# Decode attention on one core: two heads of K or V per DMA transfer, eight heads per softmax batch

## The chip, the core and the metric

One NeuronCore of a Trainium2 chip runs the whole kernel. The metric is device time in microseconds (us) of one execution, as the median of several runs. The core has five engines with a program each: TensorE (PE in the profile, its weight loads PEld) for matmuls, VectorE (DVE), ScalarE (ACT), GpSimd (POOL) and SyncE (SP), which here only issues DMA transfers. Sixteen DMA engines move data from HBM into the on-chip memory SBUF, which has 128 partitions; matmuls write to PSUM.

## The reference

A decoder block for four sequences with one new token each. x is 4 x 576.

```python
q = layernorm(x) @ wq                      # 32 query heads of 128
k = k_cache[:, :, Sk - W:, :]              # 4 x 16 KV heads, last W = 4096 of 16384 positions
v = v_cache[:, :, Sk - W:, :]
p = softmax(q @ k.T * 128 ** -0.5)         # two query heads share a KV head
h = x + (p @ v) @ wo
n = layernorm(h)
out = h + (relu(n @ W_gate) * (n @ W_up)) @ W_down   # F = 4608
```

All tensors are bf16. Per KV head the window of K is 4096 x 128 values, 1 MB, and it lies in one piece in HBM; the same holds for V. There are 64 KV heads (4 sequences x 16), so K and V are 128 MiB (134.2 million bytes) of the 159.6 million that the kernel reads; the rest are the five weight matrices and x.

## The kernel before

The order of the work is written out by hand. Each engine has its own program, and a small scheduler (class Sched) turns named events into semaphore waits.

**SP** issues every large transfer in one fixed list, in order. Before each it waits for whoever used the buffer last, so a wait holds up everything behind it in the list. The list is: wq in five pieces (L205 to L208); then for m = 0, 1, 2 ... K of head m and V of head m - 5 (L209 to L213; VLEAD is 5); then wo (L214), W_gate and W_up (L218 to L227) and W_down (L230 to L236). K goes through a ring of 6 buffers and V through one of 10, in the SBUF tensor `pool`; a buffer has 4608 columns of bf16. wq occupies the first five V buffers. A K or V transfer is 1 MB: 128 partitions with 8 KB each, and partition p holds positions 32p to 32p + 31 of one head (L195 to L203). A K buffer comes free with the transpose of that head, event ("TR", i), a V buffer with the last matmul on it, ("PV", i).

**DVE** transposes each K head in 32 x 32 blocks of 4-byte words into one of three buffers kT (`tr`, L376). It waits for the K transfer and, from the fourth on, for the matmuls that read the kT buffer before.

**PE** computes scores (`qk`, L497): eight matmuls of 512 columns per head, with a stationary operand qz that holds the queries of the head in its own columns and zeros elsewhere, so four heads (a batch, NB = 4) accumulate into the same 128 x 1024 of PSUM (`sc`, two of them in turn), row 32g + 2r + h for head r of the batch and query h.

For a **batch** DVE takes the maximum over the row (`rmax`, L384), POOL takes the maximum over partitions (L268), DVE makes the bias (`fbias`, L391), ACT writes the exponentials P (L314, two instructions of 512 columns), DVE transposes P (`trp`, L397) and ACT casts it to bf16 as `prob` (L321). PE then multiplies prob with V (`pv`, L514): eight matmuls of 512 columns per head with eight rows of output. In PE's program the PV of head j stands after the scores of head j + 6 (PVLAG, L539). ACT copies the batch's result out of PSUM (L301), and PE picks the right blocks out of it (`ext`, L526). ACT fills qz for the batch after next (`qzero`, L285).

Before the first head there is a chain of setup. POOL clears qz (L254) and then builds an identity matrix (L255). DVE makes masks from it (L345 to L363), ACT the normalised x (L281), PE its transpose (L476) and then q; the first transpose of K stands behind this in DVE's program (L413), and the second behind the copies of q (L415 to L417).

After the last head come wo, the second layernorm, the gate and up matmuls (each waits for its own weights) and the down matmuls. W_down lands on the place of K and wo buffers, so its transfers wait for the last wo matmul (event "ATTN", L234).

Of the kernel before, what the change touches and what calls it, by code (L numbers as in the profile page):

```python
# [12 lines left out]
B = 4  # L13
# [6 lines left out]
T = WIN // 128  # L20
# [3 lines left out]
NPAIR = B * KVH  # L24
NB = 4
NBATCH = NPAIR // NB
# [3 lines left out]
SLOT = 4608  # L30
NKS = 6
NVS = 10
NSLOT = NKS + NVS
# [3 lines left out]
PVLAG = 6  # L37
# [63 lines left out]
def bass_sequential_preLN__sliding_block_cached__glu_gated_reglu__decode_kernel(  # L101
# [12 lines left out]
    with ExitStack() as es:  # L114
# [4 lines left out]

        pool = sb("pool", [128, NSLOT, SLOT], BF16)  # L120
        kT = sb("kT", [128, NKT, WIN // 2], FP32)
# [19 lines left out]
        qz = sb("qz", [128, 2, NB, 4, 128], BF16)  # L141
        mask = sb("mask", [128, 4, 2 * NB], FP32)
        selT = sb("selT", [128, 4, 2 * NB], FP32)
        rmx = sb("rmx", [128, 2], FP32)
        pmax = sb("pmax", [128, 2, 2 * NB], FP32)
        bcm = sb("bcm", [128, 2, 2 * NB], FP32)
        t8 = sb("t8", [128, 2 * NB], FP32)
# [5 lines left out]
        prob = sb("prob", [128, 3, NB, T, 2], BF16)  # L153
# [22 lines left out]

        rings = {"K": [list(range(NKS)), 0], "V": [list(range(NKS, NSLOT)), 0]}
        slot_user = {}
        transfers = []
        slot_of = {}  # L180

        def add(name, ring, consumer, make, fixed=None):
            if ring is not None:
                slots, i = rings[ring]
                s = slots[i % len(slots)]
                rings[ring][1] += 1
                free = slot_user.get(s)
                slot_user[s] = consumer
                key = f"slot{s}"
            else:  # L190
                s, free, key = fixed, None, "fix_" + str(name).replace("'", "").replace("(", "").replace(")", "").replace(", ", "_")
            slot_of[name] = s
            transfers.append((name, key, free, lambda e, s=s: make(e, s)))

        def kv(cache, i):  # L195
            b, kvh = divmod(i, KVH)
            return cache[b, kvh, SK - WIN:SK, :].rearrange("(p t) d -> p (t d)", p=128)

        def add_K(i):
            add(("K", i), "K", ("TR", i), lambda e, s: e.dma_start(out=pool[:, s, 0:WIN], in_=kv(A_k_cache, i)))  # L200

        def add_V(i):
            add(("V", i), "V", ("PV", i), lambda e, s: e.dma_start(out=pool[:, s, 0:WIN], in_=kv(A_v_cache, i)))  # L203

        for c in range(4):  # L205
            add(("wq", c), "V", "QMM", lambda e, s, c=c: e.dma_start(out=pool[:, s, 0:H * DH], in_=A_wq[c * 128:(c + 1) * 128, :]))
        add(("wq", 4), "V", "QMM", lambda e, s: e.dma_start(out=pool[:, s, 0:H * DH // 2],
                                                            in_=A_wq[512:576, :].rearrange("r (u n) -> (r u) n", u=2)))  # L208
        for m in range(NPAIR + VLEAD):  # L209
            if m < NPAIR:  # L210
                add_K(m)
            if m >= VLEAD:
                add_V(m - VLEAD)  # L213
        for g in range(NWO):  # L214
            add(("wo", g), "K", "ATTN",
                lambda e, s, g=g: e.dma_start(out=pool[:, s, :].rearrange("p (q x) -> p q x", q=2),  # L216
                                              in_=A_wo[g * 1024:(g + 1) * 1024, :].rearrange("(q p e) n -> p q (e n)", q=2, e=4)))
        for c in range(4):  # L218
            for kind, W in (("wg", B_W_gate), ("wu", B_W_up)):
                add((kind, c), "V", None,  # L220
                    lambda e, s, c=c, W=W: e.dma_start(out=pool[:, s, 0:F], in_=W[c * 128:(c + 1) * 128, :]))

        s4 = rings["V"][0][rings["V"][1] % NVS]
        for u, (kind, W) in enumerate((("wg", B_W_gate), ("wu", B_W_up))):
            transfers.append(((kind, 4), f"gu4_{u}", slot_user[s4],
                              lambda e, u=u, W=W: e.dma_start(out=pool[:, s4, u * HALF:(u + 1) * HALF],
                                                              in_=W[512:576, :].rearrange("r (u n) -> (r u) n", u=2))))  # L227
        wd_sb = pool[:, 0:NKS, :].rearrange("p s x -> p (s x)")[:, 0:FC * D].rearrange("p (g x) -> p g x", g=NG)
        WD = [(0, GD * JJ), (GD * JJ, 2 * GD * JJ)] + [(g * JJ, (g + 1) * JJ) for g in range(2 * GD, NG - 1)] + [(FC - JJ, FC - 1), (FC - 1, FC)]
        for k, (f0, f1) in enumerate(WD):  # L230
            g0, j0 = divmod(f0, JJ)
            g1, nj = (f1 // JJ, JJ) if f1 - f0 >= JJ else (g0 + 1, f1 - f0)
            transfers.append((("wd", k), f"wd{k}", "ATTN",
# [8 lines left out]
        def prog_sync(S):  # L242
            for name, key, free, make in transfers:
                S.dma("sync", make, key, deps=[free], name=land(name))
            S.dma("sync", lambda e: e.dma_start(out=out.rearrange("b s d -> (b s) d"), in_=out_sb[:, :]), "outdma",
                  deps=["OUT0", "OUT1"], name="STORED")
            S.wait("sync", "STORED")
# [24 lines left out]
        def prog_act(S):  # L272
# [12 lines left out]
            def qzero(n):  # L285
                b, q = divmod(n, 4)
                for g in range(4):
                    deps = []
                    if g == 0:
                        deps = ["D_QR", "QZ0"] if n < 2 else [("QK", NB * (n - 2) + NB - 1)]  # L290
                    src = bass.AP(tensor=qrep, offset=32 * g * 4 * H * B + 8 * q * B + b, ap=[[4 * H * B, 32], [2 * B, NB], [H * B, 4], [B, 2]])
                    dst = bass.AP(tensor=qz, offset=32 * g * 2 * NB * 512 + (n % 2) * NB * 512 + 32 * g,
                                  ap=[[2 * NB * 512, 32], [512 + 2, NB], [128, 4], [1, 2]])
# [11 lines left out]
            for n in range(NBATCH):  # L305
                for half in range(2):
                    deps = []
                    if half == 0:
# [5 lines left out]
                    S.op(a, lambda e, n=n, half=half: e.activation(  # L314
                        out=P[:, half * 512:(half + 1) * 512], in_=sc[n % 2][:, half * 512:(half + 1) * 512], func=ACT.Exp,
                        scale=SCALE, bias=bias[:, n % 2:n % 2 + 1], accum_out=rs2[:, n % 2, half:half + 1]),
                        deps=deps, name=("EXP", n) if half else None, signal=half == 1)
                deps = [("TRP", n)]
                if n >= 3:
                    deps.append(("PV", NB * (n - 3) + NB - 1))  # L320
                S.op(a, lambda e, n=n: e.copy(out=prob[:, n % 3, :, :, :],  # L321
                                              in_=probT[:, :, 0:2 * NB].rearrange("p t (r h) -> p r t h", h=2)), deps=deps, name=("CMP", n))
# [13 lines left out]
        def prog_dve(S):  # L336
# [17 lines left out]
            for x in range(2):  # L354
                S.op(v, lambda e, x=x: e.memset(pb[PVB + x], 0.0), name=f"PVZ{x}")  # L355
            S.op(v, lambda e: e.tensor_reduce(out=mask[:, 0, :], in_=ident_b[:, :].rearrange("p (r u) -> p u r", u=2 * NB), axis=AX.X, op=ALU.add),
                 name="M0")
            S.op(v, lambda e: e.tensor_reduce(out=mask[:, 3, :], in_=bass.AP(tensor=ident_b, offset=0, ap=[[128, 128], [1, 2 * NB], [32, 4]]),
                                              axis=AX.X, op=ALU.add), name="M3")
            S.op(v, lambda e: e.tensor_scalar(out=mask[:, 1, :], in0=mask[:, 0, :], scalar1=2 * BIG, scalar2=-BIG, op0=ALU.mult, op1=ALU.add),  # L360
                 deps=["M0"], name="M1")
            S.op(v, lambda e: e.tensor_scalar(out=mask[:, 2, :], in0=mask[:, 0, :], scalar1=-2 * BIG, scalar2=BIG, op0=ALU.mult, op1=ALU.add),
                 name="M2")  # L363
            S.op(v, lambda e: e.reciprocal(out=st1[:, 5:6], in_=st1[:, 4:5]), deps=["A_STD"], name="D5")
# [11 lines left out]
            def tr(i):  # L376
                deps = [land(("K", i))]
                if i >= NKT:
                    deps.append(("QK", i - NKT))
                src = pool[:, slot_of[("K", i)], 0:WIN].bitcast(FP32).rearrange("p (t c k) -> p c t k", c=2, k=32)  # L380
# [3 lines left out]
            def rmax(n):  # L384
                S.op(v, lambda e: e.tensor_reduce(out=rmx[:, n % 2:n % 2 + 1], in_=sc[n % 2][:, :], axis=AX.X, op=ALU.max),  # L385
                     deps=[("QK", NB * n + NB - 1)], name=("RMAX", n))
# [4 lines left out]
            def fbias(n):  # L391
                S.op(v, lambda e: e.scalar_tensor_tensor(out=t8[:, :], in0=bcm[:, n % 2, :], scalar=-SCALE, in1=mask[:, 2, :],  # L392
# [4 lines left out]
            def trp(n):  # L397
                S.op(v, lambda e: e.transpose(out=probT[:, :, :].rearrange("p t j -> p (t j)"), in_=P[:, :]),  # L398
                     deps=[("EXP", n)] + ([("CMP", n - 1)] if n >= 1 else []), name=("TRP", n))
                b, q = divmod(n, 4)  # L400
                S.op(v, lambda e: e.tensor_tensor(out=rs1[:, n % 2:n % 2 + 1], in0=rs2[:, n % 2, 0:1], in1=rs2[:, n % 2, 1:2], op=ALU.add),  # L401
                     name=("RS1", n))
                S.op(v, lambda e: e.tensor_scalar(out=rowsum[:, b, 8 * q:8 * q + 8], in0=mask[:, 3, :], scalar1=rs1[:, n % 2:n % 2 + 1],
                                                  scalar2=None, op0=ALU.mult), deps=[("RS1", n)], name=("RSUM", n))

            def norm(b):
# [3 lines left out]
                     deps=[("RS", b), ("EXT", 4 * b + 3)], name=("NORM", b))  # L410

            for i in range(NPAIR):
                tr(i)  # L413
                if i == 0:
                    S.op(v, lambda e: e.tensor_copy(out=qT_sb[:, :], in_=pb[QB][:, 0:H * B]), deps=["QMM"], name="D_QT")  # L415
                    S.op(v, lambda e: e.tensor_copy(out=qrep[:, :, :].rearrange("p c x -> p (c x)"), in_=pb[QR]), deps=["QREP"], name="D_QR")  # L416
                    S.op(v, lambda e: e.tensor_copy(out=selT[:, :, :].rearrange("p t (r h) -> p t r h", h=2),  # L417
                                                    in_=bass.AP(tensor=ident_f, offset=0, ap=[[128, 128], [2, 4], [32, NB], [1, 2]])),
                         deps=["IDF"], name="SELT")
                n, pos = divmod(i, NB)  # L420
                if pos == NB - 1:
                    rmax(n)
                if pos == 0 and n >= 1:
                    fbias(n - 1)
                if pos == 1 and n >= 1:
                    trp(n - 1)
# [38 lines left out]
        def prog_pe(S):  # L465
# [73 lines left out]
            for i in range(NPAIR + PVLAG):  # L539
                if i < NPAIR:  # L540
                    qk(i)
# [100 lines left out]
```

## Time and profile before

| what | value |
|---|---|
| median of 3 runs | 389.33 us (389.22 to 389.44) |
| the profiled execution, its time | 389.34 us |
| its span in the profile | 387.6 us |
| bytes read from HBM | 159.58 MB |
| busy: PE, DVE, ACT, POOL | 301.1, 204.6, 60.1, 10.7 us |
| 64 transposes of K, mean of one | 2305 ns |
| 512 score matmuls, 512 PV matmuls, mean of one | 416 ns, 393 ns |
| a K or V transfer, from issue to landing (median) | 26.1 us, 26.9 us |

The span is the profile's own; 1.7 us of the execution's time lie around it. The strip of 40 slices shows each engine's busy share in tenths, and below it what the DMA engines moved in GB/s, so each slice is 9.7 us. The page's share of busy time counts a matmul from its start to its modelled end, so several overlap and PE's number is the union. "Releaser" names what ended an engine's wait. The lists of packets count every piece that a DMA engine moved: one for each partition's contiguous run, and a 4-byte one for each engine and transfer, which sets the semaphore.

### The profile page before, as it was taken

To read this page: it belongs to the slowest core of one execution; us is meant where nothing else is said; L and a number is where in the kernel's file an instruction comes from. 1 tells how busy PE (TensorE), PEld (TensorE's weight loads), DVE (VectorE), ACT (ScalarE), POOL (GpSimd) and SP (SyncE) were. 2 spreads that over 40 slices of the span, in tenths; PEclk is the share of its full clock that TensorE was granted. 3 is DMA by queue.
4 is the path that set the end of the run, shared out by engine and by line. 5 is a ranking of instruction groups with operands and counts; after the bars stand their busy time and mean duration, and the time that the engine had idled before them with its cause. 6 is when DMAs were issued, how large, how long until landed. Compare 5 with 4: busy or idle time off the path is not lost.

```text
span 387.6 us, 4471 instructions
## 1 busy us (share of the span) xinstructions
PE 301.1 (78%) x1906; PEld 131.3 (34%) x1906; DVE 204.6 (53%) x228; ACT 60.1 (16%) x173; POOL 10.7 (3%) x28
## 2 busy tenths in 40 slices
PE   0078779797979797979787878796879798774477
PEld 0053224242424242324232323242323233364344
DVE  0265967658483856574748575656566665011000
ACT  4020212111111111111111111111111111200000
POOL 3000000000000000000000000000000000000000
PEclk9999699999989998989999999899989989875559
DMA  8999999999999999999999999999999999999995
GB/s 322 419 419 423 423 421 418 420 423 420 423 419 420 424 421 422 420 420 421 421 424 421 418 424 421 424 417 421 421 421 422 423 421 419 414 418 421 418 412 203
DMA packets 23524, 159.88 MB, mean 413 GB/s; under 512 B 2505, under 2 KB 2641, under 8 KB 5585
## 3 DMA queue, kind: packets, MB, share of 16 engines
q1 hardware_dynamic: 23496, 159.59, 99.3%
q8 instruction: 15, 0.25, 0.3%
q14 instruction: 5, 0.03, 0.0%
q10 hardware_dynamic: 8, 0.00, 0.0%
HBM read 159.58 MB, written 0.00 MB: 412 GB/s over the span
## 4 chain that ended last, share of the span: by engine, by line
DMA 55%; PE 26%; DVE 12%; issue 4%; SPq 1%; ACT 0%; POOL 0%; POOLq 0%
DMA pool<-in_A_k_cache_dram 42%; PE sc L469 15%; PE pb L469 11%; DVE kT L382 8%; DMA pool<-in_B_W_down_dram 7%; DMA pool<-in_A_wo_dram 6%; DVE rmx L385 2%; SPq L216 1%; DVE pmax L387 0%; DVE pb L355 0%; ACT qz L294 0%; ACT xn_bf L281 0%; DVE sel L346 0%; PE pb L476 0%; DVE qrep L416 0%
## 5 line engine op out<-in xcount | busy, mean ns | idle before, releaser
L382 DVE STREAM_TRANSPOSE kT<-pool 128x2048 f32<-128x2048 f32 x64 | 147.2, 2305 | 59.5 <-DMA pool<-in_A_k_cache_dram 59.3
L469 PE MATMUL sc<-kT,qz 128*128 128x512 bf16 x512 | 137.8, 416 | 44.3 <-DVE t L392 33.0
L469 PE MATMUL pb<-pool,prob 128*8 128x512 bf16 x512 | 120.2, 393 | 0.0
L469 PEld LDWEIGHTS sc<-kT,qz 128*128 128x128 bf16 x512 | 47.0, 101 | 130.6 <-DVE t L392 40.5
L469 PEld LDWEIGHTS pb<-pool,prob 128*8 128x8 bf16 x512 | 38.9, 88 | 73.7 <-issue 28.2
L314 ACT ACTIVATE P<-sc,bias 128x512 f32<-128x512 f32 x32 | 21.7, 683 | 160.6 <-DVE bias L394 160.6
L385 DVE TENSOR_REDUCE rmx<-sc 128x1 f32<-128x1024 f32 x16 | 19.6, 1225 | 47.0 <-PE sc L469 47.0
L398 DVE STREAM_TRANSPOSE probT<-P 128x1024 f32<-128x1024 f32 x16 | 19.3, 1205 | 1.5 <-ACT P L314 1.5
L469 PEld LDWEIGHTS pb<-selT,cp 128*128 128x128 f32 x128 | 16.6, 191 | 6.6 <-ACT cp L301 4.2
L469 PE MATMUL pb<-selT,cp 128*128 128x8 f32 x128 | 15.4, 247 | 3.2 <-ACT cp L301 3.2
L301 ACT COPY cp<-pb 128x512 f32<-128x512 f32 x16 | 9.4, 586 | 53.5 <-PE pb L469 53.5
L469 PE MATMUL pb<-hnT,pool 128*128 128x4 bf16 x288 | 8.8, 167 | 9.8 <-DMA pool<-in_B_W_up_dram 5.2
L476 PE MATMUL pb<-ident_b,xn_bf 4*128 4x4 bf16 (+1 forms) x5 | 0.4, 175 | 19.6 <-ACT xn_bf L281 19.6
L294 ACT COPY qz<-qrep 32x32 bf16<-32x32 bf16 x64 | 13.9, 217 | 7.6 <-DVE qrep L416 7.0
L268 POOL PARTITION_ALL_REDUCE bcm<-pmax x16 | 5.9, 368 | 304.4 <-DVE pmax L387 304.4
L321 ACT CAST prob<-probT 128x256 bf16<-128x256 f32 x16 | 6.6, 414 | 44.6 <-DVE rs L401 44.6
L469 PEld LDWEIGHTS pb<-hnT,pool 128*128 128x128 bf16 x288 | 8.2, 104 | 10.3 <-DMA pool<-in_B_W_up_dram 5.4
L460 DVE TENSOR_TENSOR hhT<-pb,gate_sb 128x144 bf16<-128x144 f32 x1 | 0.3, 308 | 20.9 <-ACT gate_sb L330 20.9
L469 PE MATMUL pb<-pool,hhT 128*4 128x288 bf16 x72 | 10.0, 306 | 0.4 <-DMA pool<-in_B_W_down_dram 0.4
L469 PEld LDWEIGHTS pb<-pool,hhT 128*4 128x4 bf16 x72 | 6.3, 90 | 4.1 <-DMA pool<-in_B_W_down_dram 0.9
L469 PE MATMUL sc<-oX,pool 128*128 128x4 bf16 (+1 forms) x160 | 5.7, 170 | 1.6 <-DMA pool<-in_A_wo_dram 1.1
L476 PEld LDWEIGHTS pb<-ident_b,xn_bf 4*128 4x128 bf16 (+1 forms) x5 | 0.3, 107 | 19.6 <-ACT xn_bf L281 19.6
(93 smaller groups left out, 71.7 us busy)
## 6 DMA issues: line engine op xcount, KB each, us to landing
pool<-in_A_k_cache_dram SPq DMA_DIRECT2D x64, 1024.0 KB, 26.1
pool<-in_A_v_cache_dram SPq DMA_DIRECT2D x64, 1024.0 KB, 26.9
pool<-in_A_wo_dram SPq DMA_DIRECT2D x4, 1152.0 KB, 27.0
pool<-in_B_W_gate_dram SPq DMA_DIRECT2D x4, 1152.0 KB, 25.7
pool<-in_B_W_up_dram SPq DMA_DIRECT2D x4, 1152.0 KB, 24.4
pool<-in_A_wq_dram SPq DMA_DIRECT2D x4, 1024.0 KB, 7.9
pool<-in_B_W_down_dram SPq DMA_DIRECT2D x2, 1296.0 KB, 27.3
pool<-in_B_W_down_dram SPq DMA_DIRECT2D x5, 432.0 KB, 14.7
```

The costliest lines, as they stand in the source:

```text
L216: lambda e, s, g=g: e.dma_start(out=pool[:, s, :].rearrange("p (q x) -> p q x", q=2), in_=A_wo[g * 1024:(g + 1) * 1024, :].rearrange("(q p ...
L268: S.op(g, lambda e, n=n: e.partition_all_reduce(bcm[:, n % 2, :], pmax[:, n % 2, :], 128, bass_isa.ReduceOp.max), deps=deps, name=("PAR", n))
L294: S.op(a, lambda e, src=src, dst=dst: e.copy(out=dst, in_=src), deps=deps, name=("QZ", n) if g == 3 else None, signal=g == 3)
L301: S.op(a, lambda e: e.copy(out=cp[:, n % 2, :], in_=pb[PVB + n % 2]), deps=deps, name=("CP", n))
L314: S.op(a, lambda e, n=n, half=half: e.activation(out=P[:, half * 512:(half + 1) * 512], in_=sc[n % 2][:, half * 512:(half + 1) * 512], fun ...
L321: S.op(a, lambda e, n=n: e.copy(out=prob[:, n % 3, :, :, :], in_=probT[:, :, 0:2 * NB].rearrange("p t (r h) -> p r t h", h=2)), deps=deps, ...
L382: S.op(v, lambda e: e.transpose(out=dst, in_=src), deps=deps, name=("TR", i))
L385: S.op(v, lambda e: e.tensor_reduce(out=rmx[:, n % 2:n % 2 + 1], in_=sc[n % 2][:, :], axis=AX.X, op=ALU.max), deps=[("QK", NB * n + NB - 1 ...
L398: S.op(v, lambda e: e.transpose(out=probT[:, :, :].rearrange("p t j -> p (t j)"), in_=P[:, :]), deps=[("EXP", n)] + ([("CMP", n - 1)] if n ...
L460: S.op(v, lambda e: e.tensor_tensor(out=hhT[:, :, :], in0=pb[GUB][:, FC * B:2 * FC * B].rearrange("p (f b) -> p f b", b=B), in1=gate_sb[:, ...
L469: S.op(t, lambda e: e.matmul(o, lhsT=l, rhs=r, start=start, stop=stop, skip_group_check=skip), deps=deps, name=name, signal=name is not None)
L476: S.op(t, lambda e, c=c, w=w, src=src, base=base: e.transpose(out=tpv[0:w, base + c * 4:base + (c + 1) * 4], in_=src[0:B, c * 128:c * 128 ...
```

## The change

K and V of two neighbouring heads of one sequence (a "duo") come in one transfer of 2 MB. The 128 partitions hold the two heads in turn: partition 2p + s holds positions 64p to 64p + 63 of head s, 16 KB in one piece. There are 4 K buffers and 4 V buffers of that size in `pool`, which is now addressed by offsets; the weights overlay them, and a transfer waits for every event whose buffer it overlaps. The list still runs K of duo m, V of duo m - 5.

A duo's transpose is done in two halves (64 transposes of the same shape as before), each with eight score matmuls, four for each head; since a column of kT now belongs to one head by its parity, the matmuls take every other word. A batch has eight heads (four duos) and eight batches replace sixteen. Scores of a batch fill the same 128 x 1024 of PSUM, now 16 rows of queries per group of 32. The exponentials are written twice, once for each parity (P has twice the columns), and the cast to prob multiplies by 0 or 1 per partition (`par`), so that the rows of the other head are zero. PV then takes a whole duo: 16 matmuls of 512 columns with 16 rows of output, twice as many per step and half as many steps. PVLAG is 5 duos, prob has two buffers instead of three. The bias is computed directly after the maximum, not after the next transpose. qz and its clearing by POOL are twice as large.

```diff
-T = WIN // 128
+T = WIN // 64
-NPAIR = B * KVH
+NDUO = B * KVH // 2
-NBATCH = NPAIR // NB
+NBATCH = NDUO // NB
+NHB = 4 * NB
-NKS = 6
-NVS = 10
+DUO = 2 * WIN * DH // 128
+NKS = 4
+NVS = 4
-PVLAG = 6
+PVLAG = 5
-        qz = sb("qz", [128, 2, NB, 4, 128], BF16)
+        qz = sb("qz", [128, 2, 2 * NB, 4, 128], BF16)
-        prob = sb("prob", [128, 3, NB, T, 2], BF16)
+        prob = sb("prob", [128, 2, NB, T, 4], BF16)
-        def kv(cache, i):
-            b, kvh = divmod(i, KVH)
-            return cache[b, kvh, SK - WIN:SK, :].rearrange("(p t) d -> p (t d)", p=128)
+        def duo(cache, d):
+            b, m = divmod(d, KVH // 2)
+            return cache[b, 2 * m:2 * m + 2, SK - WIN:SK, :].rearrange("s (p t) d -> p s (t d)", p=64)
+        def add_K(d):
+            s = d % NKS
+            add(("K", d), f"kslot{s}", s * DUO, DUO, ("TR", 2 * d + 1),
+                lambda e, o: e.dma_start(out=o, in_=duo(A_k_cache, d)))
+        def add_V(d):
+            s = d % NVS
+            add(("V", d), f"vslot{s}", (NKS + s) * DUO, DUO, ("PV", d),
+                lambda e, o: e.dma_start(out=o, in_=duo(A_v_cache, d)))
...
-                    S.op(a, lambda e, n=n, half=half: e.activation(
-                        out=P[:, half * 512:(half + 1) * 512], in_=sc[n % 2][:, half * 512:(half + 1) * 512], func=ACT.Exp,
+                    S.op(a, lambda e, n=n, th=th: e.activation(
+                        out=P[:, th * 1024:(th + 1) * 1024].rearrange("p (x u) -> p x u", u=2),
+                        in_=bass.AP(tensor=sc[n % 2], offset=th * 512, ap=[[1024, 128], [1, 512], [0, 2]]), func=ACT.Exp,
...
-                S.op(a, lambda e, n=n: e.copy(out=prob[:, n % 3, :, :, :],
-                                              in_=probT[:, :, 0:2 * NB].rearrange("p t (r h) -> p r t h", h=2)), deps=deps, name=("CMP", n))
+                for s in range(2):
+                    S.op(a, lambda e, n=n, s=s: e.activation(out=prob[:, n % 2, :, :, 2 * s:2 * s + 2],
+                                                             in_=probT[:, :, 0:NHB].rearrange("p t (r s h) -> p s r t h", s=2, h=2)[:, s, :, :, :],
+                                                             func=ACT.Copy, scale=par[:, s:s + 1]),
+                         deps=deps if s == 0 else [], name=("CMP", n) if s else None, signal=s == 1)
...
+            S.op(v, lambda e: e.tensor_reduce(out=t8[:, NHB:NHB + 1], in_=mask[:, 1, :], axis=AX.X, op=ALU.max), deps=["M1"], name="CAP0")
+            S.op(v, lambda e: e.tensor_scalar(out=t8[:, NHB:NHB + 1], in0=t8[:, NHB:NHB + 1], scalar1=0.0, scalar2=None, op0=ALU.max), deps=["CAP0"], name="CAP")
...
-                deps = [land(("K", i))]
+                deps = [land(("K", i // 2))]
+                x0 = at[("K", i // 2)] + (i % 2) * (DUO // 2)
...
-                kv_ = kT[:, i % NKT, :].bitcast(BF16).rearrange("p (x e) -> p x e", e=2)
+                kv_ = kT[:, i % NKT, :].bitcast(BF16).rearrange("p (c x s e) -> p c x s e", c=2, s=2, e=2)
...
-                        mm(sc[n % 2][:, half * 512:(half + 1) * 512], qz[:, n % 2, pr, ce, :], kv_[:, x0:x0 + 512, e],
+                        mm(pb[2 * (n % 2) + th], qz[:, n % 2, 2 * r + s, ce, :], kv_[:, c, :, s, e],
...
-                    mm(pb[PVB + n % 2][32 * pr:32 * pr + 8, :], prob[:, n % 3, pr, 4 * tg:4 * tg + 4, :].rearrange("p t h -> p (t h)"),
-                       pool[:, s, tg * 512:(tg + 1) * 512], tg == 0, last,
+                    mm(pb[PVB + n % 2][32 * r:32 * r + 16, :], prob[:, n % 2, r, 4 * tg:4 * tg + 4, :].rearrange("p t h -> p (t h)"),
+                       pool[:, x0 + tg * 512:x0 + (tg + 1) * 512], tg == 0, last,
...
-            for i in range(NPAIR + PVLAG):
-                if i < NPAIR:
-                    qk(i)
+            for i in range(NDUO + PVLAG):
+                if i < NDUO:
+                    qk(2 * i)
+                    qk(2 * i + 1)
```

## The prediction

> **What bounds the kernel now.** I read the page's strip first, then the chain that ended last.
>
> ```profile
> DMA  8999999999999999999999999999999999999995
> GB/s 322 419 419 423 423 421 418 420 423 420 423 419 420 424 421 422 420 420 421 421 424 421 418 424 421 424 417 421 421 421 422 423 421 419 414 418 421 418 412 203
> ...
> DMA 55%; PE 26%; DVE 12%; issue 4%; SPq 1%; ACT 0%; POOL 0%; POOLq 0%
> ```
>
> The DMA engines are full from the second slice to the last but one, at 420 GB/s, and DMA holds most of the chain. PE's 26% there is the first 130 us, where the chain happens to be followed through compute; the rate is the same. What compute is worth is read from the steady stretch, 100 to 300 us, first the engines, then DVE's waits from 60 to 320 us (total, times, longest):
>
> ```profile
> 100.00:300.00 200.00, 169.89 (x738) 65.77 (x736) 123.30 (x116) 33.38 (x105) 3.66 (x10) 0.96 1.01 421
> ```
> ```profile
> DVE kT L382 <- DMA pool<-in_A_k_cache_dram: 56.6, 31, 3.4
> ```
>
> PE is busy 85% and DVE 62%, while DMA is at 1.01, and DVE's transposes wait for K. So the time is bytes over rate, plus a head and a tail. An edit to compute counts only if it stops the stream; a change of the stream's rate counts in full.
>
> **The rate: what a packet costs.** K and V are 134.2 MB, and at 420.6 GB/s they take 319.1 us. A transfer of 1 MB is 128 packets of 8 KB and 16 of 4 bytes; a duo of 2 MB is 128 packets of 16 KB and the same 16. So 16384 - 8192 data packets and 2048 - 1024 small ones go: 9216 packets, 576 per DMA engine. What one is worth I take from two stretches of different packet size. Here is the queue view from 100 to 300 us, K and V alone (packets, MB, share of 16 engines), and then that from 376 to 382 us, W_down in pieces of 3456 bytes and less:
>
> ```profile
> DMA packets 11561, 84.24 MB, mean 421 GB/s; under 512 B 1285, under 2 KB 1285, under 8 KB 1285
> ...
> q1 hardware_dynamic: 11553, 84.12, 101.1%
> ```
> ```profile
> q1 hardware_dynamic: 837, 2.37, 97.7%
> ```
>
> Engine time is 16 x 200 x 1.011 = 3235.2 us in the first and 16 x 6 x 0.977 = 93.8 us in the second. With a ns for each packet and c us for each MB: 11553a + 84.12c = 3235.2 and 837a + 2.37c = 93.8 (a in us). That gives c = 37.75 us per MB and a = 5.2 ns. I take this, since it is fitted to the kernel's own two extremes: 576 x 5.2 ns = 3.0 us less, which is a stream of 424.6 instead of 420.6 GB/s.
>
> Bounds: by throughput alone (417 GB/s for W_down's 3456-byte pieces from 375 to 380 us, so 132.6 ns a piece, and 420.6 for 8 KB, 311.6 ns) the fixed part is some 2.0 ns, so 1.1 us less. The trace's 4-byte packets last 9.5 ns; if all of that is fixed, 5.5 us less. Below nothing: the weights' 9216-byte packets (340 to 370 us, mixed with 4608 bytes) move at 419, not above 421, so longer packets need not be faster; and here neighbouring partitions read places 4 MiB apart, which no transfer of this trace does.
>
> [...] Heads here lie 4 MiB apart. [...] No run here shows such a pitch.
>
> **The start.** K now has 4 buffers, so the fifth K waits for the second transpose of the first duo, and everything on SP queues behind it. Timeline of the first 30 us (start, duration):
>
> ```profile
> 0.89 3.52 POOL L254 MEMSET qz<- 128x4096 bf16 x1
> ...
> 15.35 0.28 POOL L255 TENSOR_SCALAR_AFFINE_SELECT ident_b<-ident_b 128x128 bf16<-128x128 bf16 x1 [10.95 <-issue]
> ...
> 21.13 2.30 DVE L382 STREAM_TRANSPOSE kT<-pool 128x2048 f32<-128x2048 f32 x1
> ...
> 26.48 4.50 DVE L382 STREAM_TRANSPOSE kT<-pool 128x2048 f32<-128x2048 f32 x2
> ```
>
> The second transpose ends at 28.8. POOL clears twice as much qz, 3.5 us more, and then sits 10.95 us before it builds the identity matrix on which everything waits. If that pause starts after the clearing (as its place in POOL's order says), all of this moves by 3.5 us; if it runs from launch, by nothing. Two small DVE instructions (CAP0, CAP) and a wider selT add 0.3. So K of duo 4 is issued between 29.1 and 32.6. From SP's first issue at 0.73 to a full stream is 1.6 us (227 GB/s over the first 5 us means a start at 2.3), so its data come at 30.7 to 34.2. What is queued before it, wq and four K duos, 13.1 MB, is through at 33.6 (387 GB/s to 30.0, then 421), or 33.4 with the faster packets. The hole is 0 to 0.8 us; I take 0.8, since the chain shows POOL's pause only behind the clearing. The next K is due when duo 4 is in, at 39.2 in that case; it waits for the fourth transpose, two of 2.3 us later, 37.2, and starts at 38.8. It just fits, and from then two transfers come for each wait.
>
> **Steady state: covers.** A duo's two transfers take 9.97 us.
> - PE per duo: two groups of eight score matmuls (1.98 us each in the timeline at 277 us), 16 PV matmuls (2 x 1.89), a quarter of 1.06 for the selection: 8.0 us. Halving the selections, row maxima (1.23), copies (0.59) and POOL's maxima removes some work, which is worth nothing under the stream.
> - Softmax of a batch, from the last K's landing: two transposes 4.6, scores 2.0, maximum 1.2 + 0.2, to the bias 0.9 (286.0 to 288.9 in the trace holds a transpose besides), exponentials over 1024 (0.68 for 512; between 0.7 and 1.4 each, I take 1.2, and 0.2 to read the sum): 2.8, a transpose in front and one of P at the size of K's 4.6, two casts of 0.41 to 0.82: 1.6. Sum 18 us. The batch's first V lands five transfers later, 24.9 us. If those 7 us of cover are gone, PV is late, and V's buffers still hold.
> - A V buffer is refilled four duos on, with seven transfers between: 34.9 us, less 1.6 to start. PV ends some 8 us after landing. K is freed 5 to 8 us after landing, with the same 34.9. SP's waits therefore end long before the queue is empty.
> - New is the step of the score matmuls' moving operand: 8 bytes instead of 4. Bounds: a group of eight at 1.98 us (step 4) against 1.89 (PV, step 2) says nothing or 5%; if time goes with the step, it doubles. I take 5%, and keep both ends.
>
> **The end.** V's last PV is 16 matmuls, 1.9 us more than now, so the wo matmuls end up to 1 us later than 348.3 and W_down is issued at 349.3. Behind it the queue holds work to 370, so 20 us hide that. After the last weight lands nothing changes.
>
> **Sum**, against the profiled execution (389.34, span 387.6 and 1.7 around it; the median is 389.33, the same): 389.3 - 3.0 + 0.8 = 387.1 us.
>
> **Rivals.**
> 1. The rate does not move: cost goes with bytes, or the long runs are cut into 8 KB pieces again. For: 419 GB/s at 9216 bytes. Then -1.1 (or 0) and 0 to 0.8 at the start: 388.2 to 390.1, say 389.2.
> 2. The stream slows, because two rows 4 MiB apart alternate within each DMA engine. For: no row shows it. [...] At the rate of the slowest slices, 412 to 415, K and V take 323.4 us or more: +4.3 + 0.8 = 394.4. It decides as soon as the rate is under 420.
> 3. The score matmuls become the bound by their step. PE has 9.97 - 8.0 = 2.0 us per duo to spare, so a group must go from 1.98 to 2.95 us before it counts. If it doubles, each duo takes 2.0 us more: 32 x 2.0 = 64, 451 us. Against: from step 2 to 4 it cost at most 5%.
> 4. All 9.5 ns are fixed and the start has no hole: 389.3 - 5.5 = 383.8.
>
> **Chances.** Forecast 0.52, rival 1 0.16, rival 2 0.14, rival 3 0.09, rival 4 0.09. The range 384.2 to 393.0 leaves out rival 3, half of rival 2 and part of rival 4: 0.20. A measurement here can tell 0.2%, 0.8 us, from no change; faster (under 388.5) is the forecast and rival 4, 0.61; slower (over 390.1) rivals 2 and 3, 0.23; between them 0.16.
>
> **What would show it.** Right: 9216 packets fewer, 424 to 425 GB/s from 100 to 300 us, one weak slice near 34 us, PE and DVE with the same kind of waits. Wrong: as many packets as before (rival 1); a rate of 420 or less with DMA still at 1.0 (1, 2); DMA under 1.0 in steady state, with DVE waiting for PE and score groups over 2.9 us (3). A hole of several us after 33 us would mean that I misjudged the start.

## The result, and the profile after

The changed kernel takes 461.54 us against 389.34 before: 1.186 times as long, 95% interval 1.184 to 1.188. The forecast of 387.1 us was wrong, and so was its range; rival 3, to which I gave 0.09, named what happened and 451 us.

The page after, in the order in which I read the page before: strips, chain, and the costliest group.

```profile
DMA  8989998998789978997898888987996444699996
GB/s 336 429 374 388 429 431 323 400 412 355 290 357 394 385 254 344 395 377 296 364 387 361 345 341 347 390 347 306 363 388 252 182 183 182 250 406 421 420 413 253
...
PE 63%; issue 15%; DVE 11%; DMA 6%; ACT 4%; POOL 1%; POOLq 0%
...
L479 PE MATMUL sc<-kT,qz 128*128 128x512 bf16 x512 | 236.9, 630 | 22.0 <-DVE kT L394 20.1
```

The same group on the page before:

```profile
L469 PE MATMUL sc<-kT,qz 128*128 128x512 bf16 x512 | 137.8, 416 | 44.3 <-DVE t L392 33.0
```

The DMA strip has holes all the way, and the chain went from 55% DMA to 63% PE. The score matmuls hold PE for 236.9 us instead of 137.8. In some early slices, while V buffers are still free, the stream shows 429 and 431 GB/s, more than any slice before: the faster stream is there, and unused. The steady stretch, 100 to 300 us, has PE at 95%, the DMA engines at 0.88 and the stream at 353 GB/s:

```profile
100.00:300.00 200.00, 189.74 (x573) 56.80 (x571) 94.00 (x69) 22.58 (x47) 1.94 (x5) 0.97 0.88 353
```

The timeline at the end of a batch shows the two parts of the loss (start, duration, and in brackets the idle time before and what ended it):

```profile
199.84 3.62 PE L479 MATMUL pb<-pool,prob 128*16 128x512 bf16 x16
199.95 1.23 DVE L397 TENSOR_REDUCE rmx<-sc 128x1 f32<-128x1024 f32 x1 [12.17 <-PE sc L479]
...
202.25 2.30 DVE L394 STREAM_TRANSPOSE kT<-pool 128x2048 f32<-128x2048 f32 x1
...
204.61 3.77 PE L479 MATMUL sc<-kT,qz 128*128 128x512 bf16 x8 [1.15 <-DVE kT L394]
204.70 2.31 DVE L410 STREAM_TRANSPOSE probT<-P 128x2048 f32<-128x2048 f32 x1
...
207.23 8.89 DVE L394 STREAM_TRANSPOSE kT<-pool 128x2048 f32<-128x2048 f32 x4
209.59 3.77 PE L479 MATMUL sc<-kT,qz 128*128 128x512 bf16 x8 [1.21 <-DVE kT L394]
```

First, eight score matmuls take 3.77 us; before they took 1.98 (the prediction's reading at 277 us). Second, PE sits idle twice, 2.4 us in all, because DVE has had the kT buffers free for a while but does the maximum and the bias first, and then the transpose of P ahead of the next transpose of K. A duo comes every 11.9 us (the four of the batch from 199.95 to 247.68 in the chain) where a stream of 428 GB/s would give one every 9.8.

### The profile page after: what moved, and what is told of

It is laid out like the page before. It is cut to its first block, busy times and chain, and to the rows that moved or that the text cites. A ratio compares the mean times of both kernels' runs of the same rounds, so it can differ in the third digit from the quotient of the medians.

```text
span 461.0 us, 4134 instructions
## 1 busy us (share of the span) xinstructions
PE 393.8 (85%) x1842; PEld 137.0 (30%) x1842; DVE 189.6 (41%) x174; ACT 50.0 (11%) x101; POOL 11.3 (2%) x20
## 4 chain that ended last, share of the span: by engine, by line
PE 63%; issue 15%; DVE 11%; DMA 6%; ACT 4%; POOL 1%; POOLq 0%
PE sc L479 41%; PE pb L479 21%; DMA pool<-in_B_W_down_dram 6%; DVE probT L410 4%; ACT P L319 4%; DVE kT L394 3%; DVE rmx L397 2%; POOL bcm L272 1%; DVE pmax L399 0%; DVE rowsum L415 0%; ACT prob L328 0%; DVE t L404 0%; DVE bias L406 0%; ACT cp L306 0%; ACT qz L299 0%
## 5 line engine op out<-in xcount | busy, mean ns | idle before, releaser
L479 PE MATMUL sc<-kT,qz 128*128 128x512 bf16 x512 | 236.9, 630 | 22.0 <-DVE kT L394 20.1
L479 PE MATMUL pb<-pool,prob 128*16 128x512 bf16 x512 | 117.3, 392 | 0.0
L479 PEld LDWEIGHTS sc<-kT,qz 128*128 128x128 bf16 x512 | 55.6, 114 | 189.3 <-issue 156.0
L479 PEld LDWEIGHTS pb<-pool,prob 128*16 128x16 bf16 x512 | 43.6, 92 | 78.7 <-issue 26.6
L397 DVE TENSOR_REDUCE rmx<-sc 128x1 f32<-128x1024 f32 x8 | 9.8, 1225 | 93.8 <-PE sc L479 93.8
L319 ACT ACTIVATE P<-sc,bias 128x1024 f32<-128x1024 f32 x16 | 17.7, 1110 | 251.1 <-DVE bias L406 251.1
L410 DVE STREAM_TRANSPOSE probT<-P 128x2048 f32<-128x2048 f32 x8 | 18.5, 2311 | 3.4 <-ACT P L319 2.5
L328 ACT ACTIVATE prob<-probT,par 128x512 bf16<-128x512 f32 x16 | 11.2, 750 | 19.0 <-DVE rs L413 19.0
L479 PE MATMUL pb<-selT,cp 128*128 128x16 f32 x64 | 8.0, 257 | 3.5 <-ACT cp L306 3.5
L479 PEld LDWEIGHTS pb<-selT,cp 128*128 128x128 f32 x64 | 8.4, 195 | 8.0 <-ACT cp L306 4.5
```

The lines of the kernel that those rows point to most:

```text
L319: S.op(a, lambda e, n=n, th=th: e.activation(out=P[:, th * 1024:(th + 1) * 1024].rearrange("p (x u) -> p x u", u=2), in_=bass.AP(tensor=sc ...
L328: S.op(a, lambda e, n=n, s=s: e.activation(out=prob[:, n % 2, :, :, 2 * s:2 * s + 2], in_=probT[:, :, 0:NHB].rearrange("p t (r s h) -> p s ...
L479: S.op(t, lambda e: e.matmul(o, lhsT=l, rhs=r, start=start, stop=stop, skip_group_check=skip), deps=deps, name=name, signal=name is not None)
```

## The experiments

Theory S: the 8-byte step of the score matmuls' moving operand is the cause. Rival O: the order at the batch ends. Rival B: buffers too few, or a slower stream.

**e1_step4**, the step alone undone; each matmul now mixes columns of the two heads.

```diff
-                kv_ = kT[:, i % NKT, :].bitcast(BF16).rearrange("p (c x s e) -> p c x s e", c=2, s=2, e=2)
+                kv_ = kT[:, i % NKT, :].bitcast(BF16).rearrange("p (c s x e) -> p c s x e", c=2, s=2, e=2)
...
-                        ... kv_[:, c, :, s, e],
+                        ... kv_[:, c, s, :, e],
```

> The changed kernel, but the score matmuls read their 512 columns at a step of 4 bytes instead of 8 (so they mix the columns of the two heads of a duo; the output is not the reference's, the amount of work is the same). Theory S, the step is the cause: a group of eight score matmuls falls from 3.7 to about 2.0 us, PE needs 8.0 us per duo and the stream decides again: K and V at the 431 GB/s that the changed kernel shows where nothing holds it (311 us instead of 319), less the hole at the start of some 3 us: 382 to 387 us. Rival O, the new order at the batch ends (maximum, bias, two transposes with PE idle) is the cause: the groups may get faster, but the time stays above 430. Rival B, four buffers of 2 MB are too few: the stream stays under 400 GB/s from 100 to 300 us and the time above 430.

Measured: 387.30 us, 0.9956 of before (0.9934 to 0.9978). Groups of eight take 1.98 us again, and the strip and the queue view from 100 to 300 us (packets, MB, share) show the stream back:

```profile
119.58 1.98 PE L479 MATMUL sc<-kT,qz 128*128 128x512 bf16 x8 [1.15 <-DVE kT L394]
```
```profile
GB/s 315 434 424 383 388 431 432 423 429 427 429 429 423 429 432 429 422 429 427 429 427 429 427 427 426 431 431 422 429 431 431 422 427 432 405 418 421 417 413 175
```
```profile
DMA packets 5870, 85.54 MB, mean 428 GB/s; under 512 B 649, under 2 KB 649, under 8 KB 649
...
q1 hardware_dynamic: 5864, 85.45, 100.4%
```

S holds, O and B fall as sole causes: nothing else of the change was undone. At 428 GB/s, above every slice of before, two heads 4 MiB apart on alternate partitions do not slow the stream (rival 2 of the prediction). The time is 0.3 us above what I expected; the slices of 383 and 388 show a hole at the start.

**e2_step8_old**, the step alone done, in the kernel before.

```diff
-                kv_ = kT[:, i % NKT, :].bitcast(BF16).rearrange("p (x e) -> p x e", e=2)
+                kv_ = kT[:, i % NKT, :].bitcast(BF16).rearrange("p (x e) -> p x e", e=4)
...
-                        ... kv_[:, x0:x0 + 512, e],
+                        ... kv_[:, half * 512:(half + 1) * 512, ce],
```

> The kernel before, but its score matmuls read their 512 columns at a step of 8 bytes instead of 4 (each matmul gets a quarter of the words of both halves; the output is not the reference's, the amount of work is the same). Transfers, buffers, batches and order are those of before. Theory S: groups of eight take 3.7 us, PE needs 2 x 3.7 + 3.8 + 0.5 = 11.7 us for two heads where the stream gives 9.97, so 32 x 1.75 = 56 us more, 440 to 455 us. Rivals O and B: 389 us, unchanged.

Measured: 475.56 us, 1.220 of before (1.217 to 1.224), 20 us over the expectation. PE's longest wait says where these come from (total, times, longest):

```profile
PE sc L469 <- DVE t L392: 33.0, 15, 3.8
```

The kernel before has this very row, 33.0 us in 15 waits at its batch ends. There the stream covers it. If it is paid in full here, 475.6 - 33.0 = 442.6 us are left, inside what was expected for the matmuls alone; no run takes these waits out of this kernel, but e7_order does it in the changed one. So S is right for the step, and O has a point that I had left out: once PE is the bound, its waits at batch ends add up.

**e3_steps**, the price of each step, in the kernel before.

```diff
-                kv_ = kT[:, i % NKT, :].bitcast(BF16).rearrange("p (x e) -> p x e", e=2)
+                kv_, step = kT[:, i % NKT, :].bitcast(BF16), n // 2 + 1
...
-                        ... kv_[:, x0:x0 + 512, e],
+                        ... kv_[:, 0:511 * step + 1:step],
```

> The kernel before, but the step of the score matmuls' moving operand is 2 bytes in the first two batches, 4 in the next two and so on up to 16 bytes in the last two (all read from the start of the buffer; the output is not the reference's). It prices the step: what eight matmuls take at 2, 4, 6 ... 16 bytes. [...] If time goes with the step, 16 bytes take twice as long as 8, 7.4 us. Rivals O and B: all alike, 2.0 us.

Measured (545.94 us, one run). One group of eight from PE's timeline for each step of 2, 4, 6 ... 16 bytes; the second number is its duration:

```profile
50.91 1.90 PE L469 MATMUL sc<-kT,qz 128*128 128x512 bf16 x8
65.65 1.98 PE L469 MATMUL sc<-kT,qz 128*128 128x512 bf16 x8
109.37 2.88 PE L469 MATMUL sc<-kT,qz 128*128 128x512 bf16 x8
155.75 3.77 PE L469 MATMUL sc<-kT,qz 128*128 128x512 bf16 x8
209.98 4.67 PE L469 MATMUL sc<-kT,qz 128*128 128x512 bf16 x8
258.53 5.57 PE L469 MATMUL sc<-kT,qz 128*128 128x512 bf16 x8
334.29 6.45 PE L469 MATMUL sc<-kT,qz 128*128 128x512 bf16 x8
429.06 7.36 PE L469 MATMUL sc<-kT,qz 128*128 128x512 bf16 x8
```

Up to 4 bytes the step is nearly free. From there each 2 bytes add 0.9 us to 4096 columns, so the time goes with the bytes stepped over, (7.36 - 1.98) / 12 / 4096 = 0.11 ns per byte and column. The time does not level off from 8 bytes on. The granted clock is not behind the row: it averaged 0.97 from 130 to 180 us (8 bytes) and 0.66 from 380 to 500 us, where PV groups took up to 3.58 us instead of 1.89, yet all eight groups of a step from 6 bytes on agree within 0.02 us but the first at 6 bytes, and each step adds the same. At 8 bytes the group takes 1.9 times as long as at 4; why, no run shows.

**e7_order**, the other part of the loss: the changed kernel with its 8-byte step, other order on DVE.

```diff
-                if pos == 2 * NB - 1:
+                if pos == 1 and n >= 1:
-                    rmax(n)
-                    fbias(n)
-                if pos == 0 and n >= 1:
+                    rmax(n - 1)
+                    fbias(n - 1)
+                if pos == 2 and n >= 1:
                     trp(n - 1)
...
+            rmax(NBATCH - 1)
+            fbias(NBATCH - 1)
```

> The changed kernel with its 8-byte step, but in DVE's program the next batch's first two transposes stand ahead of the row maximum, and the third ahead of the transpose of P, so that PE need not wait for DVE at the end of a batch (2.4 us of PE idle at each of eight batch ends). All of the reference is computed. Theory S: PE stays the bound with 7.4 + 3.6 + 0.3 us per duo; the eight waits give back at most 19 us: 442 to 450 us. Rival O, the order at the batch ends is the cause: 400 or less.

Measured: 435.39 us, 1.118 of before (1.115 to 1.120), less than I expected. PE's busy time from 100 to 300 us is now the whole stretch:

```profile
100.00:300.00 200.00, 200.00 (x621) 61.48 (x619) 105.16 (x72) 25.45 (x55) 1.54 (x4) 1.00 0.95 385
```

So the waits were worth 461.5 - 435.4 = 26 us, more than the 19 that I had counted from one batch end, and the step alone, with PE not idle from 100 to 300 us, 435.4 - 387.3 = 48 us over e1. The trace of the changed kernel shows where the rest of the 26 is: all such waits of PE, then the PV group behind the second wait, and that stretch with its granted clock (the number before the last two):

```profile
PE sc L479 <- DVE kT L394: 20.1, 14, 4.8
```
```profile
213.29 4.48 PE L479 MATMUL pb<-pool,prob 128*16 128x512 bf16 x16
```
```profile
213.30:217.70 4.40, 4.40 (x17) 1.53 (x16) 2.82 (x2) 0.00 (x0) 0.00 (x0) 0.80 0.67 287
```

The waits are 20.1 us. Behind six of the seven batch ends the next PV group also takes 4.41 to 4.77 us instead of 3.62, at a granted clock of 0.75 to 0.81: 5.6 us more in all. In e7 the clock is 1.00 in the row above, and the PV groups from 100 to 360 us take 3.62. Rival O is the smaller part, and only because PE is the bound.

**e4_split**, a version that keeps the step at 4 bytes and computes the reference: the transpose writes the two heads apart.

```diff
-                dst = kT[:, i % NKT, :].rearrange("p (c t k) -> p c t k", c=2, k=32)
+                dst = kT[:, i % NKT, :].rearrange("p (c s t k) -> p c t k s", c=2, s=2, k=16)
```

with the score matmuls of e1_step4, which now read one head each.

> The changed kernel, whole, but the transpose of K writes the two heads of a duo apart, so that the score matmuls read 512 columns of one head at a step of 4 bytes. The transpose's output goes to two places 4096 bytes apart, word by word in turn; no row prices that: 2.3 us if it costs nothing, 4.6 if it doubles. Theory S with a free transpose: as with the mixed columns, 382 to 387 us. With transposes of 4.6 us DVE needs 10.2 us per duo against 9.7 of the stream, and the time is about 400. Rivals O and B: above 430.

Measured: 398.79 us, 1.024 of before (1.022 to 1.026). The transposes' group, and the strip:

```profile
GB/s 323 420 434 304 320 443 423 418 435 424 424 428 436 425 424 426 429 431 429 423 428 429 433 426 421 428 433 433 421 426 428 263 301 317 416 418 418 422 411 221
...
L394 DVE STREAM_TRANSPOSE kT<-pool 128x2048 f32<-128x2048 f32 x64 | 234.3, 3761 | 0.4 <-PE sc L479 0.3
```

A transpose takes 3.76 us instead of 2.30. DVE then needs an estimated 8.6 us per duo (two transposes, and a quarter of the batch's maximum, bias and transpose of P), less than the stream's 9.8, and the steady slices do hold 428. The time is lost in two holes, at 30 to 50 us and at 310 to 340 us, the second perhaps because DVE's lag reaches the last V buffers.

**e5_v_only**, the half of the change that has no such step: V in duos, K head by head. The scores of a head then cover both parities, and the exponentials pick them apart.

```diff
+        def add_K(i):
+            s = i % (2 * NKS)
+            b, kvh = divmod(i, KVH)
+            add(("K", i), f"kslot{s}", s * (DUO // 2), DUO // 2, ("TR", i),
+                lambda e, o: e.dma_start(out=o, in_=A_k_cache[b, kvh, SK - WIN:SK, :].rearrange("(p t) d -> p (t d)", p=128)))
...
-                        in_=bass.AP(tensor=sc[n % 2], offset=th * 512, ap=[[1024, 128], [1, 512], [0, 2]]), func=ACT.Exp,
+                        in_=bass.AP(tensor=sc[n % 2], offset=th, ap=[[1024, 128], [2, 512], [0, 2]]), func=ACT.Exp,
...
```

> Half of the change: V comes by duos of 2 MB with heads on alternate partitions, batches of eight, exponentials written for both parities; K comes head by head as before (1 MB, 8 KB packets, eight buffers), so that the score matmuls keep their step of 4 bytes. All of the reference is computed. Theory S and a stream set by packet size: groups of eight at 2.0 us, and a rate between the 420.6 of 8 KB and the 428 to 431 of 16 KB packets; 67.1 MB at each is 316 us instead of 319.1, so 3 us off; K buffers come free head by head, so the hole at the start should go. 385 to 388 us. If the batches of eight or the duos of V cost anything by themselves, the time is over 390.

Measured: 387.22 us, 0.9942 of before (0.9923 to 0.9962): faster than before, as expected. From 100 to 300 us the stream (last number) runs at 424 GB/s, between 421 (all 8 KB) and 428 (all 16 KB), and there is no hole at the start (423 GB/s from 20 to 40 us):

```profile
100.00:300.00 200.00, 169.38 (x742) 67.30 (x741) 115.55 (x82) 24.81 (x51) 1.93 (x5) 0.97 1.01 424
```

Batches of eight, the doubled exponentials and V by duos show no cost under the stream.

**e6_act_split**: instead, ScalarE copies each transposed half duo so that the heads lie apart. There are two kT buffers instead of three, and two for the copies.

```diff
+            def spl(i):
+                if i >= 2 * NDUO:
+                    return
+                S.op(a, lambda e: e.copy(out=kD[:, i % NKD, :].rearrange("p (c s x) -> p c s x", c=2, s=2),
+                                         in_=kT[:, i % NKT, :].rearrange("p (c x s) -> p c s x", c=2, s=2)),
+                     deps=[("TR", i)] + ([("QK", i - NKD)] if i >= NKD else []), name=("SPL", i))
...
```

> The changed kernel, whole, with one more step: ScalarE copies each transposed half duo so that the two heads lie apart, and the score matmuls read at a step of 4 bytes. All of the reference is computed. ScalarE gets 64 copies of 2048 elements, by its row of 1.11 us for 1024 about 2.0 us each, 128 us in all beside its 50; transposes stay at 2.3 us with two buffers, and two more hold the copies. Theory S: the stream at 428 to 431 GB/s decides, 5.6 to 7.7 us less than 319.1 for K and V, and 3 to 5 us lost at the start where the fifth K waits: 384 to 390 us. If two buffers each are too few, the chain of transpose, copy and scores (2.3 + 2.0 + 2.0 per half duo) still fits twice into 9.7 us, so the stream should hold.

Measured: 393.99 us, 1.012 of before (1.005 to 1.018): out of the expectation. The copies take 2.05 us each, as reckoned, and the steady stretch runs at 428, but PE waits 57 us for copies in all:

```profile
L311 ACT COPY kD<-kT 128x2048 f32<-128x2048 f32 x64 | 129.7, 2052 | 41.8 <-PE sc L492 28.8
```
```profile
PE sc L492 <- ACT kD L311: 57.0, 27, 6.8
```

ScalarE's one program has the exponentials between the copies. The stream has holes again at the start and from 310 to 340 us, where it falls to 321 GB/s. Which of these waits weighs most I did not take apart.

**e8_start** and **e11_start_free**: the hole at the start. In both, e1_step4 with POOL's clearing of qz behind the identity matrices; e11 holds the clearing back further.

```diff
-            S.op(g, lambda e: e.memset(qz[:, :, :, :, :].rearrange("p a r c m -> p (a r c m)"), 0.0), name="QZ0")
             S.op(g, lambda e: e.affine_select(out=ident_b[:, :], in_=ident_b[:, :], pattern=[[-1, 128]],
...
                  deps=["P1"], name="IDF")
+            S.op(g, lambda e: e.memset(qz[:, :, :, :, :].rearrange("p a r c m -> p (a r c m)"), 0.0), deps=["XN41"], name="QZ0")
```

In e8 the same without `deps=["XN41"]`.

> The kernel of e1_step4 (score matmuls at a step of 4 bytes, heads mixed, so the output is not the reference's), with POOL clearing qz after it has built the identity matrices instead of before. If POOL's pause follows the clearing, the identity comes 7 us earlier, the second transpose ends near 26 instead of 33 us and the fifth K is issued before the queue runs dry: the weak stretch from 30 to 45 us goes, and 2 to 3 us with it: 384.5 to 385.5 us. If the pause runs from launch, nothing changes: 387 us.

Measured: 386.21 us, 0.9916 of before (0.9902 to 0.9929), half of what I expected. First the timeline of e1_step4, then that of e8:

```profile
18.36 0.28 POOL L259 TENSOR_SCALAR_AFFINE_SELECT ident_b<-ident_b 128x128 bf16<-128x128 bf16 x1 [10.54 <-issue]
...
19.44 0.21 DVE L359 COPY dup<-ident_b 64x128 bf16<-64x128 bf16 x1
...
24.41 2.30 DVE L394 STREAM_TRANSPOSE kT<-pool 128x2048 f32<-128x2048 f32 x1
```
```profile
11.91 0.28 POOL L258 TENSOR_SCALAR_AFFINE_SELECT ident_b<-ident_b 128x128 bf16<-128x128 bf16 x1 [10.96 <-issue]
...
12.94 7.00 POOL L267 MEMSET qz<- 128x8192 bf16 x1
12.99 7.02 DVE L359 COPY dup<-ident_b 64x128 bf16<-64x128 bf16 x1
...
24.57 2.30 DVE L394 STREAM_TRANSPOSE kT<-pool 128x2048 f32<-128x2048 f32 x1
```

The pause of 11 us does follow what stands before it in POOL's program: the identity now comes at 11.9 us instead of 18.4. But DVE's copy `dup`, 0.2 us elsewhere, lasts as long as the clearing beside it, and the first transpose starts no earlier than in e1. So the 1.1 us from e1 to e8 are not those of an earlier transpose. The stream from 35 to 45 us is better in e8 (423 and 416 GB/s against 383 and 383); why, no run shows.

> The kernel of e8_start (score matmuls at a step of 4 bytes, heads mixed, so the output is not the reference's) with the same wait for POOL's clearing. The hole at 30 to 35 us (344 GB/s there) should go: 1 to 1.5 us off 386.2, 384.5 to 385.3 us. If the copy did not wait for the clearing, 386.2.

Measured: 384.54 us, 0.9874 of before (0.9859 to 0.9889). With the clearing held back, dup takes 0.21 us, the first transpose starts at 20.0 and the slices between 30 and 45 us hold 419 to 436 GB/s. So the copy had waited for the clearing: 7.02 us beside it in e8, 0.21 us without it here. By what it was held, no run shows.

**e9_split_early** and **e10_split_free**: the whole reference again, e4_split with the order of e7_order on DVE, and with POOL's clearing as in e8 and e11.

> The kernel of e4_split (the transpose writes the two heads apart, all of the reference is computed) with two edits of order: POOL clears qz after the identity matrices, and DVE does the next batch's first two transposes ahead of the row maximum and the third ahead of the transpose of P. The transposes still take 3.8 us, so DVE needs 8.6 us per duo against 9.8 of the stream. If e4 lost its time to the hole at the start (some 5 us) and to DVE's lag at the end (some 9 us, the last transpose 20 us behind its K), both from waits that these edits remove, 383 to 388 us. If DVE's lag comes from its busy time alone, the hole at the end stays and the time is 393 or more.

Measured: 389.81 us, 1.0005 of before (0.9995 to 1.0016): a little over the expectation. The hole at the end is gone (424 to 429 GB/s from 315 to 330 us), so it came from waits and not from DVE's busy time: a transpose still takes 3.77 us. Two edits were made at once, but POOL's clearing lies at the start. The hole at the start remains (206 GB/s from 40 to 45 us).

> The kernel of e9_split_early (the transpose writes the two heads apart, all of the reference is computed), but POOL's clearing of qz also waits for DVE's last setup instruction (event XN41). In e8_start DVE's copy dup took 7.0 us, exactly as long as POOL's clearing beside it, against 0.2 us without it. If the clearing held that copy, DVE's setup now ends some 7 us earlier, the first transpose starts when the first K is in, near 20 us instead of 24.6, and the second ends near 28 instead of 34; the hole of some 5 us between 30 and 45 us shrinks to 0 to 2 and the time is 384.5 to 387 us, under that of the kernel before and of e5_v_only. If the copy waited for something else, 389.8 as before.

Measured: 386.12 us, 0.9906 of before (0.9889 to 0.9923): the lowest median here of a kernel that computes the reference, though its interval touches that of e5. Its strip, of the slowest of its executions (388.15 us), has one weak slice left at the start, and some near 330 us:

```profile
GB/s 305 440 424 419 378 429 431 431 428 427 424 429 427 428 427 426 431 426 431 427 424 431 426 431 427 427 427 424 431 429 431 417 421 388 408 420 422 415 415 146
```

## Why the prediction was wrong, point by point

- **What bounds the kernel now**: right. PE at 85% and DVE at 62% were cover, and every experiment that left them enough cover ran at the stream from 100 to 300 us.
- **The step of the score matmuls**: this is the step that failed. I took 5% and kept "doubles" as the other end; it is 1.98 to 3.77 us, 90% more (e3). The two rows that I leaned on, 2 and 4 bytes, lie on the flat part of the curve, and I read a flat part as a rule. My own break-even, 2.95 us a group, showed that the answer decided everything; two rows on one side of it were no reason for 0.09.
- **Steady state, the covers**: they were reckoned against the stream alone. With PE as the bound, DVE's order at the batch ends cost 26 us more (e7), and the edit that puts the bias directly behind the maximum, which I costed at nothing, is part of that order; what it costs by itself no run shows. Rival 3 had 64 us for the step, where 48 were measured, and nothing for these waits. That its 451 us missed by 10 only is luck: the two errors go against each other.
- **The rate**: the mechanism was right, the size was off. I took 5.2 ns per packet, 3.0 us and 424.6 GB/s; measured are 428 GB/s, 134.2 / 0.4206 - 134.2 / 0.428 = 5.5 us, which over 576 packets per engine is 9.6 ns each. That is my upper end, the 9.5 ns of a 4-byte packet. The packet records of the traces show why the fit came out too low. In the kernel before, from 376 to 382 us, packets of 1152, 2304 and 3456 bytes last 51, 93 and 135 ns: 42 ns for each 1152 bytes, and 9 ns beside. The 8 KB packets from 100 to 300 us, at 313.9 ns, lie 6 ns above that line, and I drew one line through both. In e5, where both lengths run side by side, a 16 KB packet lasts 615.3 ns, 12.5 less than two of 8 KB; so the packets' length counts, and not only that there are fewer transfers.
- **The pitch of 4 MiB**: no slowing seen in this pattern, 428 GB/s with it (e1) against 420.6 before.
- **The start**: the place was right, the size not. I took 0.8 us; taking the hole away gave 387.3 - 384.5 = 2.8 us (e1 to e11). The clearing delays the identity about as I had reckoned, 3.5 us: it comes at 19.65 in the changed kernel and at 18.36 in e1, against 15.35. Nor does the next K "just fit" in e1: the stream is weak a second time there, at 336 and 311 GB/s from 38 to 42 us. Why, no run shows.
- **The end**: nothing was seen of it; W_down came in time in all kernels at the stream.

Put together: 389.3, less 2.0 for the faster stream net of the hole (e1), plus 48 for the step, plus 26 for the waits that it uncovers, is 461. The terms are the differences from run to run (before, e1, e7, the changed kernel), so that they add up proves nothing by itself; each stands on its own run. One thing is open: without the hole the gain is 389.4 - 384.5 = 4.9 us (e11), 0.6 less than the rate gives.

## What to carry to other kernels

A layout that helps a transfer may be paid for by whoever reads it, as here, where the stream rose from 420.6 to 428 GB/s (e1) and eight score matmuls went from 1.98 to 3.77 us (the changed kernel): follow the interleaved bytes to each reader's access pattern, and price a step that no row shows by measuring it, above all when the break-even lies between the bounds. Waits that cost nothing under a full stream can have a price as soon as another engine becomes the bound, 26 us here (e7), so a rival's time must count them. Of a change that loses by one of its edges, take the part that has no such edge: V alone in 16 KB packets is 0.6% faster than before. Both with the heads set apart in the transpose are 0.9% faster, but only with DVE's order and POOL's clearing changed as well; without these edits that version was 2.4% slower (e4).

## What the runs showed of the hardware

- A matmul's moving operand in bf16: 512 columns at a step of 2 or 4 bytes cost 237 to 248 ns (an eighth of 1.90 and 1.98 us), and from there to 16 bytes each 2 bytes of step added 110 to 114 ns, up to 920 ns (e3).
- A granted clock under 1 did not show in matmuls with a long step: eight at 16 bytes took 7.36 us from 429 to 436 us at a clock of 0.74 (e3), and eight at 8 bytes 3.77 us at 0.78 as at 1.00 (changed kernel, at 209.6 and 204.6 us), while PV groups at 2 bytes took 4.48 us at 0.80 instead of 3.62.
- A transfer's packets of 16 KB instead of 8 KB raised the stream of one core from 420.6 (before) to 428 GB/s (e1); half and half gave 424 (e5). Side by side (e5), a packet of 16 KB lasted 615.3 ns and one of 8 KB 313.9.
- A 32 x 32 transpose whose output goes by turns to two places 4096 bytes apart took 3.76 us for 2048 columns (e4) instead of 2.30 (changed kernel).
- A 0.2 us copy on DVE lasted 7.02 us beside a GpSimd memset of 7.00 us that had started 0.05 us earlier (e8), and 0.21 us without it (e11).
